# Softplus as one ScalarE operation, and one exponential over both halves of an attention tile

## The chip, the cores and the metric

One core of a Trainium2 chip runs the kernel. The metric is the device time of one execution in microseconds (us). Engines are named as in the profile: PE (TensorE, matrix products; PEld its weight loads), DVE (VectorE), ACT (ScalarE), POOL (GpSimd), SP (SyncE, which issues most DMAs).

## The reference

Windowed attention with 8 memory positions, then two dense layers over all 3072 tokens, all in fp32:

```python
for c in range(768 // 32):            # chunks of 32 queries, context 16 left, 8 right, and memory
    scores = scale * q_c @ k_full.T
    a = np.exp(scores - scores.max(-1))
    out_c = a / (a.sum(-1) + 1e-9) @ v_full
x = out.reshape(3072, 512)
h = x @ w_in                           # 512 x 2048
g = np.maximum(h, 0) + np.log1p(np.exp(-np.abs(h)))    # softplus
x = g @ w_out
h = x @ w_in2
g = np.maximum(h, 0) + alpha * np.minimum(h, 0)
return g @ w_out2
```

## The kernel before

**Tiling.** Attention works on 24 tiles of 128 tokens. A tile has two halves (`u` = 0, 1) of 64 queries; in each half the 8 heads lie as 4 pairs on 128 partitions, with 96 keys per query. The first dense layer goes over the tokens in 7 blocks of 4, 3, 3, 3, 4, 3 and 4 tiles (512 or 384 columns) and over the inner dimension in 16 pieces; a **step** is one piece of one block, 112 steps in all. The first two blocks each do the first 8 pieces before either does the second 8. The second dense layer follows, from about 700 us on, with a scheme of fewer products (`quad`, `out2`); the change doesn't touch it. fp32 products are made of three products of a rounded high part and a low part, so every operand is split: a cast on ACT writes the high part, a subtraction on DVE or POOL the low part.

**A step.** `pe_h` (L297) makes 12 products into a PSUM bank of `ps_h`, which has two. `act_first` (L312 to L321) computes softplus: on ACT the absolute value, the exponential and the logarithm (L312, L313, L318); the addition of one on ACT in the first 32 steps (L315) and on DVE later (L317); then three operations on DVE (L319 to L321), the last of which reads the PSUM bank again and so frees it. `act_split` casts (L328, ACT) and subtracts (L329, DVE); `pe_out` (L339) makes 12 products more into four accumulators.

**An attention tile.** `tile_plan` spreads a tile over six half-steps: scores of half 0 (products L197, then four reductions on DVE, L209, which also give the row's maximum); scores of half 1 beside the exponentials of half 0 (L219: 4 per half, on ACT, each with its sum); the norms (L228 to L230, DVE); the transposes (L237, PE, copied by ACT, L239); the values (L250, with the cast L256 and the subtraction L257). The score buffers `s` come from a pool of two; the first four tiles use space in the weight pool. The first block's four tiles run before the first step. The tiles of the second block start three half-steps apart, those of later blocks 7 or 11.

**Weights.** They come as float64 words. For each of 32 half pieces of a layer `conv_a` (L103, ACT) takes the absolute value of the high word, `conv_b` (L112, L113, L117, L120, DVE) builds fp32 from both words, and `split_w` casts (L129, ACT) and subtracts (L130, POOL). The first layer's conversions lie beside the first steps, the second layer's (`split_to`, L141, L142) from the third block on.

**Order.** Each function is put at a half-step by hand (`put`), and a scheduler orders each engine's queue from there by its own estimate of times; each engine then works its queue in order. An activation table that serves exponential and logarithm is loaded ahead of everything (L594).

Of the kernel before, what the change touches and what calls it, by code (L numbers as in the profile page):

```python
# [7 lines left out]
F32 = mybir.dt.float32  # L8
F32R = mybir.dt.float32r
I32 = mybir.dt.int32  # L10
# [6 lines left out]
P = 128  # L17
# [5 lines left out]
SW = 96  # L23
# [30 lines left out]
def attention_mlp_mlp_kernel(ctx: ExitStack, tc, qk, v, w1, w2, consts, out):  # L54
# [45 lines left out]

    def conv_a(layer, k, step=None):
        m = tpool.tile([P, DM], F32, tag="word", name="word", bufs=2)
        i = nc.scalar.activation(out=m, in_=raws[layer, k][:, :, 1].bitcast(F32), func=AF.Abs)  # L103
        pin(i, step)
        words[layer, k] = m

# [72 lines left out]
    def load_v(t):  # L179
        if t >= NT:  # L180
            return
        if t < BLOCKS1[0]:
            room = wpool.tile([P, 4 * DM], F32, tag="w", name="v0")
            v_t[t] = room[:SW, :2 * DM]
            s_room[t] = [room[:, 2 * DM + u * DM:][:, :NPAIR * SW].rearrange("p (g k) -> p g k", g=NPAIR) for u in range(2)]
        else:
            v_t[t] = apool.tile([SW, 2 * DM], F32, tag="v", name="v", bufs=1)
        nc.sync.dma_start(out=v_t[t], in_=v[t])

    def a_scores(t, u):  # L190
# [9 lines left out]
            )  # L200
        i = t % TPB
        m = mask[2 * u + (i == (TPB - 1 if u else 0))]
        if t < BLOCKS1[0]:
            s = s_room[t][u]
        else:
            s = apool.tile([P, NPAIR, SW], F32, tag="s", name="s_sb")
        nm = apool.tile([P, NPAIR], F32, tag="nm", name="nm")
        for g in range(NPAIR):
            nc.vector.tensor_tensor_reduce(  # L209
                out=s[:, g, :], in0=ps[:, g, :], in1=m, op0=ALU.add, op1=ALU.min,  # L210
                scale=-1.0 / float(D) ** 0.5, scalar=BIG, accum_out=nm[:, g:g + 1],
            )
        st[t, u] = (s, nm)

    def a_exp(t, u):
        s, nm = st[t, u]
        sm = apool.tile([P, NPAIR], F32, tag="sm", name="sm")
        for g in range(NPAIR):
            nc.scalar.activation(  # L219
                out=s[:, g, :], in_=s[:, g, :], func=AF.Exp, scale=-1.0,  # L220
                bias=nm[:, g:g + 1], accum_out=sm[:, g:g + 1],
            )
        st[t, u] = (s, sm)

    def a_norm(t, u):
        s, sm = st[t, u]
        r = apool.tile([P, NPAIR, 1], F32, tag="r", name="r")
        nc.vector.tensor_scalar(out=sm, in0=sm, scalar1=1e-9, scalar2=None, op0=ALU.add)  # L228
        nc.vector.reciprocal(out=r[:, :, 0], in_=sm)
        nc.vector.tensor_tensor(out=s, in0=s, in1=r.to_broadcast([P, NPAIR, SW]), op=ALU.mult)  # L230
        st[t, u] = s

    def a_transpose(t, u):
        s = st.pop((t, u))
        ps = ps_a.tile([SW, NPAIR, P], F32, tag="pa", name="ps_t")
        for g in range(NPAIR):
            nc.tensor.transpose(ps[:, g, :], s[:, g, :], ident)  # L237
        pt_t[t, u] = apool.tile([SW, NPAIR, P], F32, tag="pt", name="pt")
        nc.scalar.copy(out=pt_t[t, u], in_=ps)  # L239

# [18 lines left out]
    def tile_plan(t, b, c, first):  # L259

        plan = [
            (0, lambda: a_scores(t, 0)),
            (1, lambda: (a_exp(t, 0), a_scores(t, 1), load_qk(t + ahead(t)))),
            (2, lambda: (a_norm(t, 0), a_exp(t, 1))),
            (3, lambda: (a_transpose(t, 0), a_norm(t, 1))),
            (4, lambda: a_transpose(t, 1)),
            (5, lambda: (a_values(t, x_of(0, b), c), load_v(t + ahead(t)))),
        ]
        return [(first + s, f) for s, f in plan]

    def ahead(t):
        return 1 if t >= BLOCKS1[0] - 1 else NT
# [31 lines left out]
    def act_first(i):  # L304

        n = steps[i][4]
        ps = h_ps.pop(i)[:, :n]
        a = tpool.tile([P, N2], F32, tag="ta", name="ta", bufs=2)[:, :n]
        bt = tpool.tile([P, N2], F32, tag="tb", name="tb")[:, :n]
        lt = tpool.tile([P, N2], F32, tag="tl", name="tl")[:, :n]  # L310

        nc.scalar.activation(out=a, in_=ps, func=AF.Abs)  # L312
        nc.scalar.activation(out=a, in_=a, func=AF.Exp, scale=-1.0)  # L313
        if i < 2 * NF:
            nc.scalar.activation(out=bt, in_=a, func=AF.Identity, bias=1.0)  # L315
        else:
            nc.vector.tensor_scalar(out=bt, in0=a, scalar1=1.0, scalar2=None, op0=ALU.add)  # L317
        nc.scalar.activation(out=lt, in_=bt, func=AF.Ln)  # L318
        nc.vector.scalar_tensor_tensor(out=bt, in0=bt, scalar=-1.0, in1=lt, op0=ALU.add, op1=ALU.subtract)  # L319
        nc.vector.scalar_tensor_tensor(out=a, in0=bt, scalar=0.0, in1=a, op0=ALU.max, op1=ALU.subtract, reverse1=True)  # L320
        nc.vector.scalar_tensor_tensor(out=a, in0=ps, scalar=0.0, in1=a, op0=ALU.max, op1=ALU.add)  # L321
        g_a[i] = a

    def act_split(i):
# [266 lines left out]
    put(last + 28, lambda: load_w_out(1))  # L591
    put(last + 30, lambda: load_w_out(2))

    nc.scalar.preload_act_table_set("natural_log_exp_and_others")  # L594
    load_qk(0)
    load_raw(0, 0)
    nc.sync.dma_start(out=cst, in_=consts)
# [98 lines left out]
```

## Time and profile before

| | |
|---|---|
| median of 3 runs | 1202.24 us (1198.3 to 1203.86) |
| the profiled execution | 1200.04 us, its span 1198.3 us |
| mean granted clock of PE | 0.994 |
| first layer's first product, second layer's first product | about 32 us, about 650 us among the last steps |

Everything in the profile is read against the span of the one profiled execution. Busy time is the time in which an engine had an instruction; a busy share is an average over stages that have different limits. An idle time is put down to what ended last before the engine went on.

### The profile page before, as it was taken

The page shows a single profiled execution, that of the slowest core. Times are in us where ns is not written, and L with a number is a line of the kernel's source. Part 1 is how long each engine was busy: PE and PEld are TensorE (multiplying, and loading weights), DVE is VectorE, ACT ScalarE, POOL GpSimd, SP SyncE. Part 2 cuts the span into 40 slices and gives each one's busy share as a digit, 9 for nine tenths or more (in the row PEclk, how much of TensorE's full clock was granted, in tenths as well). Part 3 has the DMA queues.
Part 4 walks back from the last instruction along what each step waited for, and adds up shares of the span by engine and source line. Part 5 has one row for each costly group of instructions (what it writes and reads, how often), then busy time and mean ns, then how long its engine had stood idle before and what let it go on. Part 6 is the DMA issues. An engine that isn't in the chain of part 4 may idle for free.

```text
span 1198.3 us, 17139 instructions
## 1 busy us (share of the span) xinstructions
PE 1149.5 (96%) x6192; PEld 983.0 (82%) x6192; DVE 852.0 (71%) x1792; ACT 560.9 (47%) x1297; POOL 187.1 (16%) x148
## 2 busy tenths in 40 slices
PE   6898989989999999999999999999999999999997
PEld 6677868989999878899888888887888878888876
DVE  6999895878888888788868775567446565555542
ACT  7878665766766666566645521124121133211121
POOL 1232330323213212013212100003000002000000
PEclk9999999999999999999999999999999999999999
DMA  9554531475374362435313564465664493744630
GB/s 323 163 179 163 174 97 18 121 211 168 118 243 160 110 202 85 154 123 194 128 62 132 168 221 174 164 253 212 233 227 160 165 354 123 251 175 158 231 147 36
DMA packets 58661, 202.98 MB, mean 169 GB/s; under 512 B 5456, under 2 KB 10064, under 8 KB 52432
## 3 DMA queue, kind: packets, MB, share of 16 engines
q1 hardware_dynamic: 57424, 200.05, 48.5%
q0 software_dynamic: 1152, 1.84, 1.1%
q8 instruction: 49, 0.80, 0.3%
q14 instruction: 36, 0.29, 0.1%
HBM read 164.37 MB, written 37.49 MB: 168 GB/s over the span
## 4 chain that ended last, share of the span: by engine, by line
PE 45%; DMA 3%; DVE 2%; ACT 1%; SPq 0%; issue 0%; DVEq 0%; ACTq 0%
PE ps_o L450 20%; PE ps_q L425 18%; PE ps_hh L297 4%; PE ps_o L339 3%; DMA yraw<-y_dram 1%; DMA win<-w_in 1%; DMA out_dram<-o_sb 0%; DVE xop L401 0%; DVE ta L320 0%; DVE tp L433 0%; DVE tb L319 0%; ACT o_sb L358 0%; DVE tb L317 0%; DVE g L329 0%; SPq L382 0%
## 5 line engine op out<-in xcount | busy, mean ns | idle before, releaser
L297 PE MATMUL ps_hh<-x,wsplit 128*128 128x384 f32 (+1 forms) x1344 | 295.7, 368 | 17.1 <-DVE ta L321 15.3
L339 PE MATMUL ps_o<-g,wsplit 128*128 128x384 f32 (+1 forms) x1344 | 291.7, 362 | 3.2 <-DVE g L329 1.2
L450 PE MATMUL ps_o<-wout,g 128*128 128x512 f32 x1152 | 279.7, 392 | 3.8 <-ACT g L438 2.9
L297 PEld LDWEIGHTS ps_hh<-x,wsplit 128*128 128x128 f32 x1344 | 239.9, 190 | 46.1 <-DVE ta L321 19.6
L339 PEld LDWEIGHTS ps_o<-g,wsplit 128*128 128x128 f32 x1344 | 239.7, 188 | 27.7 <-DVE g L329 2.0
L450 PEld LDWEIGHTS ps_o<-wout,g 128*128 128x128 f32 x1152 | 216.2, 188 | 52.7 <-ACT g L438 5.4
L425 PE MATMUL ps_q<-xop,win 128*128 128x512 f32 x1008 | 245.4, 390 | 1.0 <-ACT tc L476 0.5
L425 PEld LDWEIGHTS ps_q<-xop,win 128*128 128x128 f32 x1008 | 189.2, 188 | 42.0 <-DVE xop L401 1.1
L438 ACT CAST g<-ta 128x512 fp32r<-128x512 f32 x48 | 29.9, 622 | 181.6 <-DVE ta L434 157.9
L319 DVE SCALAR_TENSOR_TENSOR tb<-tb,tl 128x384 f32<-128x384 f32 (+1 forms) x112 | 81.6, 729 | 24.6 <-ACT tl L318 23.7
L329 DVE TENSOR_TENSOR g<-ta,g 128x384 fp32r<-128x384 f32 (+1 forms) x112 | 72.5, 647 | 32.9 <-ACT g L328 32.4
L328 ACT CAST g<-ta 128x384 fp32r<-128x384 f32 (+1 forms) x112 | 62.1, 555 | 68.0 <-DVE ta L321 66.3
L320 DVE SCALAR_TENSOR_TENSOR ta<-tb,ta 128x384 f32<-128x384 f32 (+1 forms) x112 | 88.9, 794 | 1.9
L312 ACT ACTIVATE ta<-ps_hh 128x384 f32<-128x384 f32 (+1 forms) x112 | 59.4, 531 | 55.4 <-PE ps_hh L297 50.9
L318 ACT ACTIVATE tl<-tb 128x384 f32<-128x384 f32 (+1 forms) x112 | 63.6, 568 | 28.3 <-DVE tb L317 27.6
L439 DVE TENSOR_TENSOR g<-gb,g 128x512 fp32r<-128x512 f32 x48 | 34.6, 722 | 57.4 <-ACT g L438 57.4
L438 ACT CAST g<-gb 128x512 fp32r<-128x512 f32 x48 | 29.9, 622 | 92.6 <-PE ps_o L450 91.1
L433 DVE TENSOR_SCALAR tp<-ps_q,cst 128x512 f32<-128x512 f32 x48 | 35.9, 749 | 51.2 <-PE ps_q L425 51.2
L321 DVE SCALAR_TENSOR_TENSOR ta<-ps_hh,ta 128x384 f32<-128x384 f32 (+1 forms) x112 | 68.5, 611 | 2.3
L130 POOL TENSOR_TENSOR wsplit<-word,wsplit 128x512 fp32r<-128x512 f32 x32 | 50.4, 1576 | 125.2 <-ACT wsplit L129 125.2
L219 ACT ACTIVATE s_sb<-s_sb,nm 128x96 f32<-128x96 f32 x160 | 58.2, 366 | 15.8 <-DVE nm L209 15.3
L389 POOL TENSOR_TENSOR yt<-yraw 128x512 f32<-128x512 f32 x6 | 9.0, 1492 | 361.9 <-DVE xop L401 337.0
(62 smaller groups left out, 1243.9 us busy)
## 6 DMA issues: line engine op xcount, KB each, us to landing
wout<-w_out SPq DMA_DIRECT2D x48, 1024.0 KB, 6.2
raw<-in_w_dram SPq DMA_DIRECT2D x64, 512.0 KB, 4.2
win<-w_in SPq DMA_DIRECT2D x24, 1024.0 KB, 5.9
qk<-in_qk_dram SPq DMA_DIRECT2D x24, 832.0 KB, 5.1
win<-w_in SPq DMA_DIRECT2D x24, 768.0 KB, 6.4
w_in<-wst SPq DMA_DIRECT2D x24, 512.0 KB, 3.3
v<-in_v_dram SPq DMA_DIRECT2D x24, 384.0 KB, 4.8
w_out<-wst SPq DMA_DIRECT2D x16, 512.0 KB, 4.3
```

Of the source, the lines that this page charges most:

```text
L297: nc.tensor.matmul(ps[:, :n], lhsT=w[:, a, kc * P:(kc + 1) * P], rhs=x[:, c, kc, :], start=k == 0, stop=k == 3 * KD - 1,)
L312: nc.scalar.activation(out=a, in_=ps, func=AF.Abs)
L318: nc.scalar.activation(out=lt, in_=bt, func=AF.Ln)
L319: nc.vector.scalar_tensor_tensor(out=bt, in0=bt, scalar=-1.0, in1=lt, op0=ALU.add, op1=ALU.subtract)
L320: nc.vector.scalar_tensor_tensor(out=a, in0=bt, scalar=0.0, in1=a, op0=ALU.max, op1=ALU.subtract, reverse1=True)
L321: nc.vector.scalar_tensor_tensor(out=a, in0=ps, scalar=0.0, in1=a, op0=ALU.max, op1=ALU.add)
L328: anchor[i] = nc.scalar.copy(out=g[:, 0, :n], in_=a)
L329: nc.vector.tensor_tensor(out=g[:, 1, :n], in0=a, in1=g[:, 0, :n].bitcast(F32), op=ALU.subtract)
L339: nc.tensor.matmul(ps[:, :n], lhsT=w[:, a, DM + m * P:DM + (m + 1) * P], rhs=g[:, c, :n], start=first and k == 0, stop=final and k == 2,)
L425: nc.tensor.matmul(ps, lhsT=w[:, a, h * P:(h + 1) * P], rhs=x[:, c, h, :], start=first and k == 0, stop=k == 5, skip_group_check=not first,)
L438: nc.scalar.copy(out=g[:, 0, :], in_=a)
L450: nc.tensor.matmul(ps, lhsT=g[:, a, m * P:(m + 1) * P], rhs=w[:, c, :], start=f == 0 and k == 0, stop=f == NF - 1 and k == 2,)
```

## The change

`act_first` becomes one ACT operation (`Softplus`). A tile's two halves share one score buffer (of a pool of one) and one row of maxima: the maximum is now subtracted by DVE, one exponential on ACT covers both halves, one reduction on DVE makes the sums, and the norm is one chain for both. The absolute value of the weights' high word is made by two shifts on DVE. The preloading of the table is dropped. In the plan of a tile the exponential stands at half-step 2, the norm at 3 and both transposes at 4.

```diff
     def conv_a(layer, k, step=None):
         m = tpool.tile([P, DM], F32, tag="word", name="word", bufs=2)
-        i = nc.scalar.activation(out=m, in_=raws[layer, k][:, :, 1].bitcast(F32), func=AF.Abs)
+        i = nc.vector.tensor_scalar(
+            out=m.bitcast(I32), in0=raws[layer, k][:, :, 1], scalar1=1, scalar2=1,
+            op0=ALU.logical_shift_left, op1=ALU.logical_shift_right,
+        )
...
-            s_room[t] = [room[:, 2 * DM + u * DM:][:, :NPAIR * SW].rearrange("p (g k) -> p g k", g=NPAIR) for u in range(2)]
+            s_room[t] = room[:, 2 * DM:2 * DM + 2 * NPAIR * SW].rearrange("p (g k) -> p g k", k=SW)
...
-        if t < BLOCKS1[0]:
-            s = s_room[t][u]
-        else:
-            s = apool.tile([P, NPAIR, SW], F32, tag="s", name="s_sb")
-        nm = apool.tile([P, NPAIR], F32, tag="nm", name="nm")
+        if u == 0:
+            if t < BLOCKS1[0]:
+                s = s_room[t]
+            else:
+                s = apool.tile([P, 2 * NPAIR, SW], F32, tag="s", name="s_sb", bufs=1)
+            st[t] = s, apool.tile([P, 2 * NPAIR, 1], F32, tag="nm", name="nm")
+        s, nm = st[t]
...
-    def a_exp(t, u):
-        s, nm = st[t, u]
-        sm = apool.tile([P, NPAIR], F32, tag="sm", name="sm")
-        for g in range(NPAIR):
-            nc.scalar.activation(
-                out=s[:, g, :], in_=s[:, g, :], func=AF.Exp, scale=-1.0,
-                bias=nm[:, g:g + 1], accum_out=sm[:, g:g + 1],
-            )
...
+    def a_exp(t):
+
+        s, nm = st[t]
+        nc.vector.tensor_tensor(out=s, in0=s, in1=nm.to_broadcast([P, 2 * NPAIR, SW]), op=ALU.subtract)
+        nc.scalar.activation(out=s, in_=s, func=AF.Exp, scale=-1.0)
+
+    def a_norm(t):
+        s, _ = st[t]
+        sm = apool.tile([P, 2 * NPAIR], F32, tag="sm", name="sm")
+        r = apool.tile([P, 2 * NPAIR, 1], F32, tag="r", name="r")
+        nc.vector.tensor_reduce(out=sm, in_=s, axis=mybir.AxisListType.X, op=ALU.add)
         nc.vector.tensor_scalar(out=sm, in0=sm, scalar1=1e-9, scalar2=None, op0=ALU.add)
         nc.vector.reciprocal(out=r[:, :, 0], in_=sm)
-        nc.vector.tensor_tensor(out=s, in0=s, in1=r.to_broadcast([P, NPAIR, SW]), op=ALU.mult)
-        st[t, u] = s
+        nc.vector.tensor_tensor(out=s, in0=s, in1=r.to_broadcast([P, 2 * NPAIR, SW]), op=ALU.mult)
...
-            (1, lambda: (a_exp(t, 0), a_scores(t, 1), load_qk(t + ahead(t)))),
-            (2, lambda: (a_norm(t, 0), a_exp(t, 1))),
-            (3, lambda: (a_transpose(t, 0), a_norm(t, 1))),
-            (4, lambda: a_transpose(t, 1)),
+            (1, lambda: (a_scores(t, 1), load_qk(t + ahead(t)))),
+            (2, lambda: a_exp(t)),
+            (3, lambda: a_norm(t)),
+            (4, lambda: (a_transpose(t, 0), a_transpose(t, 1))),
...
-        bt = tpool.tile([P, N2], F32, tag="tb", name="tb")[:, :n]
-        lt = tpool.tile([P, N2], F32, tag="tl", name="tl")[:, :n]
-
-        nc.scalar.activation(out=a, in_=ps, func=AF.Abs)
-        nc.scalar.activation(out=a, in_=a, func=AF.Exp, scale=-1.0)
-        if i < 2 * NF:
-            nc.scalar.activation(out=bt, in_=a, func=AF.Identity, bias=1.0)
-        else:
-            nc.vector.tensor_scalar(out=bt, in0=a, scalar1=1.0, scalar2=None, op0=ALU.add)
-        nc.scalar.activation(out=lt, in_=bt, func=AF.Ln)
-        nc.vector.scalar_tensor_tensor(out=bt, in0=bt, scalar=-1.0, in1=lt, op0=ALU.add, op1=ALU.subtract)
-        nc.vector.scalar_tensor_tensor(out=a, in0=bt, scalar=0.0, in1=a, op0=ALU.max, op1=ALU.subtract, reverse1=True)
-        nc.vector.scalar_tensor_tensor(out=a, in0=ps, scalar=0.0, in1=a, op0=ALU.max, op1=ALU.add)
+        nc.scalar.activation(out=a, in_=ps, func=AF.Softplus)
...
-    nc.scalar.preload_act_table_set("natural_log_exp_and_others")
```

## Rows read from the trace of the kernel before

**Rows 1.** The page's first part: busy us, share of the span, instructions.

```profile
PE 1149.5 (96%) x6192; PEld 983.0 (82%) x6192; DVE 852.0 (71%) x1792; ACT 560.9 (47%) x1297; POOL 187.1 (16%) x148
```

**Rows 2.** Stretch, length; busy PE, PEld, DVE, ACT, POOL; PE's clock, DMA share, GB/s.

```profile
0.00:33.00 33.00, 22.84 (x241) 20.31 (x241) 23.35 (x118) 24.63 (x91) 4.02 (x7) 1.00 0.86 294
33.00:103.00 70.00, 63.51 (x415) 51.57 (x415) 69.63 (x185) 56.42 (x150) 22.36 (x15) 0.98 0.53 173
103.00:177.00 74.00, 63.74 (x343) 55.99 (x344) 68.98 (x141) 53.76 (x119) 24.25 (x15) 0.98 0.47 150
177.00:430.00 253.00, 246.63 (x1621) 229.54 (x1620) 205.89 (x511) 164.45 (x424) 61.11 (x55) 1.00 0.47 145
430.00:700.00 270.00, 266.04 (x1453) 227.07 (x1452) 213.19 (x424) 152.76 (x335) 57.14 (x45) 1.00 0.41 136
```

**Rows 3.** Waits of PE, 0 to 177 us, then 177 to 700: total, times, longest.

```profile
PE ps_hh L297 <- DVE ta L321: 8.8, 7, 2.2
...
PE ps_hh L297 <- DVE ta L321: 6.5, 9, 1.3
PE ps_x L250 <- ACT pt L239: 2.0, 1, 2.0
```

**Rows 4.** DVE by line and shape, 33 to 175 us: busy, mean ns, idle before.

```profile
L117 DVE SCALAR_TENSOR_TENSOR word<-raw,word 128x512 int32<-128x512 int32 x28 | 23.9, 854 | 0.2
...
L113 DVE TENSOR_SCALAR word<-word 128x512 int32<-128x512 int32 x27 | 14.4, 532 | 0.2
L320 DVE SCALAR_TENSOR_TENSOR ta<-tb,ta 128x512 f32<-128x512 f32 x12 | 10.8, 901 | 0.0
L319 DVE SCALAR_TENSOR_TENSOR tb<-tb,tl 128x512 f32<-128x512 f32 x12 | 10.3, 857 | 0.0
...
L321 DVE SCALAR_TENSOR_TENSOR ta<-ps_hh,ta 128x512 f32<-128x512 f32 x12 | 8.2, 680 | 0.0
L230 DVE TENSOR_TENSOR s_sb<-s_sb,r 128x384 f32<-128x384 f32 x12 | 7.7, 640 | 0.0
...
L320 DVE SCALAR_TENSOR_TENSOR ta<-tb,ta 128x384 f32<-128x384 f32 x8 | 6.6, 821 | 0.0
L321 DVE SCALAR_TENSOR_TENSOR ta<-ps_hh,ta 128x384 f32<-128x384 f32 x8 | 4.4, 548 | 0.0
L319 DVE SCALAR_TENSOR_TENSOR tb<-tb,tl 128x384 f32<-128x384 f32 x8 | 4.4, 547 | 0.0
...
L228 DVE TENSOR_SCALAR sm<-sm 128x4 f32<-128x4 f32 x12 | 2.5, 206 | 0.0
L229 DVE RECIPROCAL r<-sm 128x4 f32<-128x4 f32 x12 | 2.0, 168 | 0.0
```

**Rows 5.** All engines by line and shape, 0 to 33 us.

```profile
L219 ACT ACTIVATE v<-v,nm 128x96 f32<-128x96 f32 x32 | 11.6, 368 | 1.3 <-DVE nm L209 1.2
...
L112 DVE TENSOR_SCALAR word<-word 128x512 f32<-128x512 f32 x5 | 2.1, 420 | 8.8 <-ACT word L103 8.8
```

**Rows 6.** ACT by line and shape, 0 to 700 us.

```profile
L313 ACT ACTIVATE ta<-ta 128x384 f32<-128x384 f32 x64 | 33.5, 524 | 1.0
...
L313 ACT ACTIVATE ta<-ta 128x512 f32<-128x512 f32 x48 | 30.4, 632 | 0.9
...
L594 ACT ACT_TABLE_LOAD x1 | 1.3, 1283 | 0.7 <-PEq L686 0.7
```

**Rows 7.** Instructions in order of time, from 109 us: start, us, what.

```profile
109.09 0.66 DVE L117 SCALAR_TENSOR_TENSOR word<-raw,word 128x512 int32<-128x512 int32 x1
109.28 1.61 POOL L130 TENSOR_TENSOR wsplit<-word,wsplit 128x512 fp32r<-128x512 f32 x1 [5.46 <-ACT wsplit L129]
109.67 1.64 DVE L230 TENSOR_TENSOR s_sb<-s_sb,r 128x384 f32<-128x384 f32 x1
```

**Rows 8.** The same view, from 430 us: second half of one attention tile.

```profile
430.07 0.55 DVE L230 TENSOR_TENSOR s_sb<-s_sb,r 128x384 f32<-128x384 f32 x1
...
432.44 0.60 PE L237 MATMUL ps_t<-cst,s_sb 128*96 128x128 f32 x4
```

More of the change, by code (lines that the diff above doesn't have):

```diff
@@ L208, in a_scores @@
+        s, nm = st[t]
         for g in range(NPAIR):
+            k = u * NPAIR + g
             nc.vector.tensor_tensor_reduce(
-                out=s[:, g, :], in0=ps[:, g, :], in1=m, op0=ALU.add, op1=ALU.min,
-                scale=-1.0 / float(D) ** 0.5, scalar=BIG, accum_out=nm[:, g:g + 1],
-            )
-        st[t, u] = (s, nm)
-    def a_exp(t, u):
-        s, nm = st[t, u]
-        sm = apool.tile([P, NPAIR], F32, tag="sm", name="sm")
-        for g in range(NPAIR):
-            nc.scalar.activation(
-                out=s[:, g, :], in_=s[:, g, :], func=AF.Exp, scale=-1.0,
-                bias=nm[:, g:g + 1], accum_out=sm[:, g:g + 1],
-            )
-        st[t, u] = (s, sm)
@@ L225, in a_norm @@
-    def a_norm(t, u):
-        s, sm = st[t, u]
-        r = apool.tile([P, NPAIR, 1], F32, tag="r", name="r")
+                out=s[:, k, :], in0=ps[:, g, :], in1=m, op0=ALU.add, op1=ALU.min,
+                scale=-1.0 / float(D) ** 0.5, scalar=BIG, accum_out=nm[:, k, :],
+            )
+    def a_exp(t):
+        s, nm = st[t]
+        nc.vector.tensor_tensor(out=s, in0=s, in1=nm.to_broadcast([P, 2 * NPAIR, SW]), op=ALU.subtract)
+        nc.scalar.activation(out=s, in_=s, func=AF.Exp, scale=-1.0)
@@ L231, in a_norm @@
-        st[t, u] = s
+        nc.vector.tensor_tensor(out=s, in0=s, in1=r.to_broadcast([P, 2 * NPAIR, SW]), op=ALU.mult)
     def a_transpose(t, u):
-        s = st.pop((t, u))
+        s, _ = st[t] if u == 0 else st.pop(t)
         ps = ps_a.tile([SW, NPAIR, P], F32, tag="pa", name="ps_t")
         for g in range(NPAIR):
-            nc.tensor.transpose(ps[:, g, :], s[:, g, :], ident)
+            nc.tensor.transpose(ps[:, g, :], s[:, u * NPAIR + g, :], ident)
         pt_t[t, u] = apool.tile([SW, NPAIR, P], F32, tag="pt", name="pt")
```

## The prediction, made before the changed kernel had run

> **What bounds the kernel now.** I began with the busy shares of the page [rows 1]: TensorE (PE) is busy 96% of the span, VectorE (DVE) 71%, ScalarE (ACT) 47%. That average hides stages, so the next view is the busy time by stretch [rows 2], cut where the work changes: attention of the first block (to 33 us), conversion of the first layer's weights beside the first steps (to 177), the rest of the first layer (to 700), the second layer. PE is idle 33 - 22.84 = 10.2 us in the first stretch, 6.5 and 10.3 in the next two, 6.4 and 4.0 up to 700. The second layer has nothing that the change touches. So what can be won lies in 33 to 700 us and is 27.2 us of visible idle time, plus a little of the first stretch. DVE tells the stages apart: from 33 to 177 us it is busy 69.63 of 70 and 68.98 of 74 us, so there it is the bound; from 177 on it has about 50 us to spare in each row and only single waits cost PE time. The waits of PE name the culprit: the first product stands for a PSUM bank that the last softplus step on DVE (L321) has not yet freed, 8.8 us up to 177 and 6.5 after [rows 3].
>
> **The change part by part.** Sums are made against the profiled execution: span 1198.3, 1200.04 us in all. The median of the runs is 1202.24, 2.2 above it, within their spread.
>
> Softplus, 33 to 177 us. Per step three DVE operations go (L319 to L321) and four on ACT become one. In the stretch of [rows 4] these are 12 steps of 512 columns (10.8 + 10.3 + 8.2 = 29.3 us) and 8 of 384 (6.6 + 4.4 + 4.4 = 15.4): 44.7 us off DVE. The bank is then freed by one ACT operation of about 0.6 us (a 512-column ACT operation takes 632 ns [rows 6]) instead of by the last of seven on two queues. In these first steps the addition of one was on ACT, so nothing more leaves DVE there.
>
> Weight conversion. The absolute value of L103 moves to DVE as two shifts: 27 or so in this stretch. The trace does not have this operation. Its lower bound is the shift of L113, the same form on a packed source, 532 ns; its upper bound L117, which reads the same every-other-word source but two tensors, 854 ns [rows 4]. I take L113, because one source and one destination make it the nearer row: 27 x 0.53 = 14.4 us (23 at the upper bound). The wait for the raw weights moves with it: DVE already stood for L103 8.8 us in the first stretch [rows 5], so a wait is replaced and not added, and what is queued behind it on DVE (score reductions, norms) stood there before too.
>
> Attention. Per tile 8 exponentials with their accumulator reads become one. DVE gets a subtraction and a sum over 768 columns, its two normalising products become one of 768, its two pairs of small operations one pair. For 768 columns I extend L321: 680 ns at 512 and 548 at 384 [rows 4] give 1.03 ns a column, so 0.94 us each. Six tiles' worth lies in the stretch (12 of L230): subtraction and sum 6 x 1.88 = 11.3, product 6 x 0.94 - 7.7 = -2.1, small ones half of 2.5 + 2.0, -2.2. Together +7.0 us on DVE.
>
> So DVE's busy time falls by 44.7 - 14.4 - 7.0 = 23.3 us in a stretch that it bounds. This is the better end. The other end: durations in the rows overlap and hold collisions. L117 at 109.09 takes 0.66 but L230 begins 0.58 later, and that L230 takes 1.64 against a mean of 0.64 while GpSimd subtracts [rows 7]. GpSimd's 32 subtractions stay and will strike other operations. Counting the removed steps at 0.60 us for 512 columns and 0.47 for 384 (my estimate: the rows less 0.08 of overlap and the collisions) leaves 12 x 1.8 + 8 x 1.41 = 32.9 us removed, and with the upper bound of the shift 32.9 - 23 - 7 = 3 us gained. I take 14, about the middle, since each end rests on one of two unknowns falling one way. It can't pass the 16.8 us of visible idle time by much.
>
> First stretch, 0 to 33 us. There is no softplus here, only the added work: 5 conversions [rows 5] at 0.42 = 2.1 us, and for 4 tiles 4 x (1.88 + 0.94 - 2 x 0.64 - 0.37) = 4.7 us. DVE is busy 23.35 of the 26 us after the first data come. ACT is as full (24.63) and loses 32 exponentials at 368 ns [rows 5], but cannot give the time back, because each tile's chain now passes DVE twice more. Cost between 0 (some conversions can run later) and 6.8 us; I take 4, as the later weights still have to be converted.
>
> 177 to 700 us. DVE has room here, so the relief is worth only what PE's waits are: 10.4 us idle. The 6.5 us on L321 go. The wait for the transposes' copy (2.0 [rows 3]) stays, and waits of this kind may grow, since the tile's chain is longer by two DVE operations and both halves reach the transposes together. I take 6 gained, 0 to 10 as bounds.
>
> The rest. The score tile is one buffer of double size instead of two: a tile's score reductions must wait for the transposes of the one before. Only the second block's three tiles are planned closer (three half-steps apart) than a tile's six; behind the waiting reduction stand conversions and g's subtraction. I count this within the lower end above. The preloading of the activation table goes: its 1283 ns [rows 6] lie under the first loads, and a load put before the first exponential would cost at most that. No DMA changes its half-step.
>
> Sum: 4 - 14 - 6 = -16, so 1200.04 - 16 = 1184; with the median a little over the profiled run I say 1185.
>
> **The table rule.** The trace has a single table load, 1283 ns [rows 6]; all functions of the kernel before live in one set. The Trainium skill (ScalarE: Activation LUTs, Table sets: the hidden batching unit) says that functions are loaded in named sets and a change of set needs a load; it lists exponential and logarithm together and names no set with exponential and softplus. By its figure of 2.66 us for a switch, some 40 switches would be an estimated 106 us of ACT time. No run here shows yet which set softplus is in. The mechanism is the slower rival below. If it happens, 20 tiles lie between softplus steps, so 40 loads of 1.28 us by the row are 51 us; ACT is busy 57 to 73% of the stretches between 103 and 700 us [rows 2] and loses more than that with L313 alone (33.5 + 30.4 us [rows 6]), so its busy time does not decide, only its lateness.
>
> **The rivals.**
> A. DVE stops being the bound, and nearly all idle time between 33 and 700 us comes back: 27.2 less 4 gives 1177, and up to 10 us more where PE's matmuls now run stretched (clock 0.98 in two rows). For it: the busy-row ledger of 23 us. Against: collisions and the conversions stay. 1160 to 1177; chance 0.17.
> B. No change: the lower end of the ledger (3 gained, 6.8 lost at the start), and the later waits merely move from L321 to the transposes. About 1200, 1196 to 1208; chance 0.20. That softplus is built from several operations after all, so that little leaves the engines, ends here too (0.03 of it).
> C. Slower: PE stands at the transposes. They are placed in PE's queue early: in one tile the product ends at 430.62 and the transposes begin at 432.44, 1.8 us later [rows 8], and everything behind them (two products of a step) waits if they are late. The new chain is longer by subtraction and sum (1.88) and a table load (1.28), shorter by 4 x 0.37 - 0.85 for the exponentials (0.85 from the two sizes of L313 [rows 6]): 2.5 us. The scale tips where the lateness passes the 1.8 us of slack; 20 tiles at 0.7 us are 14 us, and 28 at twice that, with the reload for softplus behind it. From 1184 plus 14 to 28, and the start's cost at its upper end, 1208 to 1225. For it: the slack is small and DVE is a queue in order. Against: DVE and ACT are emptier, so the chain waits less in the queues. Chance 0.18.
>
> **How the numbers follow.** Forecast 0.45 (1177 to 1196, around 1185), A 0.17, B 0.20, C 0.18. A measurement of this kernel tells about 0.5%, 6 us, from no change: faster is under 1196, 0.45 + 0.17 = 0.62; same 0.20; slower 0.18. The range from 1167 to 1212 leaves out some four tenths of A and three quarters of C, 0.20.
>
> **What would show it.** Right: DVE busy in 33 to 177 us clearly below full and the waits on L321 gone with no wait of like size on softplus; the first block's first product a few us later than now; the shifts near 0.5 us; sum and subtraction near 0.95. Wrong: DVE still full to 177 us (B), transposes as PE's largest wait beside some 40 table loads (C), or the first layer's PE idle time gone (A).

## The result and the profile after

The change made the kernel slower: 1208.39 us (median of 5 runs, 1207.49 to 1211.79) against 1200.89 (5 runs, 1198.3 to 1203.86). The ratio on record is 1.0076 with an interval of 1.0052 to 1.0099; the two medians alone give 1.0062. That is 7.5 us more where 16 less were forecast; it lies inside the range, on the side that had a chance of 0.18. The profiled execution took 1211.79 us, the top of its runs, with a span of 1210.0.

The first part of the page of the changed kernel and, from its second part, the row of PE's granted clock in 40 slices (to be read against [rows 1]):

```profile
PE 1151.6 (95%) x6192; PEld 997.1 (82%) x6192; DVE 678.3 (56%) x1416; ACT 399.7 (33%) x656; POOL 172.0 (14%) x148
...
PEclk9698899979999999999999999999999999999999
```

The relief came: DVE has 174 us less to do, ACT 161. Yet PE is busy 2 us longer with the same 6192 products and idle 58.4 us, 9.6 more than before, and its clock is lower: the mean over the span is 0.972, against 0.994 before. The busy time by stretch, cut as in [rows 2] and with its columns, and then finer around the places where the loss sits:

```profile
0.00:33.00 33.00, 19.06 (x144) 17.54 (x144) 25.70 (x101) 9.50 (x14) 4.01 (x7) 0.89 0.87 293
33.00:103.00 70.00, 61.09 (x346) 49.23 (x347) 68.88 (x136) 28.75 (x46) 21.28 (x16) 0.88 0.44 145
103.00:177.00 74.00, 62.07 (x357) 56.22 (x356) 57.22 (x119) 29.38 (x49) 17.06 (x13) 0.86 0.43 141
177.00:430.00 253.00, 244.68 (x1657) 233.34 (x1657) 130.42 (x354) 109.49 (x180) 56.81 (x54) 0.97 0.46 142
...
20.00:34.00 14.00, 6.88 (x90) 6.10 (x89) 14.00 (x47) 5.20 (x9) 2.51 (x2) 0.70 0.72 226
34.00:52.00 18.00, 14.85 (x107) 11.97 (x106) 17.83 (x44) 6.57 (x12) 5.53 (x4) 0.59 0.48 164
104.00:126.00 22.00, 11.90 (x101) 10.05 (x101) 20.00 (x46) 8.87 (x14) 5.08 (x4) 0.66 0.58 194
126.00:244.00 118.00, 116.44 (x634) 107.06 (x634) 60.63 (x128) 42.33 (x73) 22.07 (x19) 0.98 0.31 85
244.00:268.00 24.00, 16.24 (x122) 14.49 (x121) 10.06 (x36) 9.74 (x15) 7.31 (x7) 0.72 0.77 210
```

Read it in two steps. In the coarse rows DVE is still full from 33 to 103 us and has air from 103 on (57.22 of 74, before 68.98). The fine rows show three holes, at 20 to 52, 104 to 126 and 244 to 268 us: PE is busy about half of the first 14 us and of the second hole, and the granted clock is 0.59 to 0.72. Between the second and third hole PE is nearly full (116.44 of 118) and DVE half empty. A *stand* is, from here on, a time in which an engine waits. What PE waited for over the whole execution, to be read against [rows 3] (total, times, longest):

```profile
PE ps_t L239 <- DVE s_sb L233: 12.1, 4, 6.2
...
PE ps_t L239 <- DVE v L233: 7.1, 2, 3.6
...
PE ps_hh L299 <- ACT ta L311: 0.6, 2, 0.5
```

The 15.3 us in which products stood for the softplus step L321 are gone, and softplus on ACT (L311) costs 0.6. In their place stand 19.2 us at the transposes (L239) for the normalising product (L233): `v` is the score space of the first block's tiles, `s_sb` the new single buffer. The instructions in order of time show the three holes. First PE and DVE in the first block, then all engines at the end of the second block's last tile, then the third block (start, us, engine, what, and in brackets the idle time before it and what ended it):

```profile
26.36 1.91 PE L239 MATMUL ps_t<-cst,v 128*96 128x128 f32 x8 [3.60 <-DVE v L233]
...
26.73 0.94 DVE L230 TENSOR_REDUCE sm<-v 128x8 f32<-128x768 f32 x1
...
29.06 0.67 DVE L123 SCALAR_TENSOR_TENSOR word<-raw,word 128x512 int32<-128x512 int32 x1
...
32.60 0.94 DVE L233 TENSOR_TENSOR v<-v,r 128x768 f32<-128x768 f32 x1
...
33.70 1.91 PE L239 MATMUL ps_t<-cst,v 128*96 128x128 f32 x8 [3.52 <-DVE v L233]
...
115.04 0.95 DVE L223 TENSOR_TENSOR s_sb<-s_sb,nm 128x768 f32<-128x768 f32 x1
115.79 1.28 ACT L224 ACT_TABLE_LOAD   x1
117.08 0.84 ACT L224 ACTIVATE s_sb<-s_sb 128x768 f32<-128x768 f32 x1
117.96 0.95 DVE L230 TENSOR_REDUCE sm<-s_sb 128x8 f32<-128x768 f32 x1 [1.37 <-ACT s_sb L224]
119.39 0.96 DVE L233 TENSOR_TENSOR s_sb<-s_sb,r 128x768 f32<-128x768 f32 x1
120.40 1.94 PE L239 MATMUL ps_t<-cst,s_sb 128*96 128x128 f32 x8 [6.23 <-DVE s_sb L233]
...
251.69 0.26 DVE L215 CUSTOM_DVE_ANT_0 s_sb<-ps_s,cst 128x96 f32<-128x96 f32 x1 [3.20 <-PE ps_t L239]
...
253.38 1.15 PE L252 MATMUL ps_x<-pt,v 96*64 96x64 f32 x32
...
259.79 1.94 PE L239 MATMUL ps_t<-cst,s_sb 128*96 128x128 f32 x8 [5.26 <-DVE s_sb L233]
...
261.66 1.98 PE L252 MATMUL ps_x<-pt,v 96*64 96x64 f32 x32
```

At the start one tile's sum begins at 26.73 and its product ends at 33.54: 6.8 us for four operations that last 2.2, because other work stands between them in DVE's queue: conversions (L123, at 29.06, and two more), the next tile's subtraction and sum, and the low parts of `x`. At 115 us the chain is bare: subtraction, table load, exponential, sum, norm, product, one after the other, and PE stands 6.23 us. At 251 us the single buffer shows itself: the reductions of the next tile (L215) stand 3.20 us until the transposes of the tile before have read `s_sb`, and then the bare chain again keeps PE for 5.26. The clock is in the last lines: the same 32 products of L252 take 1.15 us before this stand and 1.98 after it.

The same places in the kernel before, in the fine cut (its lines have the same columns):

```profile
20.00:34.00 14.00, 9.78 (x142) 8.14 (x141) 11.59 (x50) 12.04 (x43) 1.27 (x1) 1.00 0.75 228
34.00:52.00 18.00, 16.32 (x105) 13.36 (x105) 17.73 (x52) 15.96 (x47) 5.55 (x5) 0.91 0.66 228
...
104.00:126.00 22.00, 19.79 (x132) 18.24 (x133) 20.80 (x58) 17.94 (x51) 5.39 (x4) 0.92 0.55 185
...
244.00:268.00 24.00, 20.93 (x145) 19.97 (x144) 18.18 (x53) 13.85 (x40) 5.44 (x6) 1.00 0.86 222
```

A table of milestones, the starts of single products read from PE's rows in order of time (us), for the runs that the explanation uses. A step's end is given by the start of its last product, which lasts some 0.4 us:

| | first product | step 7, last | step 8, first | step 23, last | step 32, first | step 111, last |
|---|---|---|---|---|---|---|
| before | 32.3 | 112.1 | 94.5 | 204.8 | 235.8 | 699.4 |
| after | 45.3 | 106.7 | 125.9 | 212.6 | 265.3 | 709.5 |
| e1, two score buffers | 46.2 | 108.7 | 121.8 | 208.5 | 253.8 | 695.1 |
| e3, Softplus alone | 34.0 | 97.8 | 103.9 | 193.4 | 233.6 | 684.5 |
| e5, e1 with the old first block | 33.6 | 98.9 | 101.2 | 190.6 | 232.6 | 675.0 |
| e8, Exp and Ln, old attention | 33.9 | 94.7 | 99.7 | 185.1 | 227.0 | 666.8 |

Step 8 is the second block's first, and the kernel before begins it while step 7 still runs; step 32 is the third block's first. After starts 13.0 us late and has made that good by the end of step 7 (5.4 us ahead). It loses it again before step 8, which begins 31.4 us later than before, and before step 32 (29.5 later).

### The profile page after: what moved, and what is told of

Its sections match the earlier page's. It is cut to its first block, busy times and chain, and to the rows that moved or that the text cites. A ratio compares the mean times of both kernels' runs of the same rounds, so it can differ in the third digit from the quotient of the medians.

```text
span 1210.0 us, 16069 instructions
## 1 busy us (share of the span) xinstructions
PE 1151.6 (95%) x6192; PEld 997.1 (82%) x6192; DVE 678.3 (56%) x1416; ACT 399.7 (33%) x656; POOL 172.0 (14%) x148
## 4 chain that ended last, share of the span: by engine, by line
PE 75%; DVE 12%; DMA 8%; issue 2%; ACT 2%; POOL 1%; SPq 0%; ACTq 0%; POOLq 0%; DVEq 0%
PE ps_o L440 20%; PE ps_q L415 18%; PE ps_o L329 16%; PE ps_hh L299 16%; DMA yraw<-y_dram 2%; PE ps_s L200 2%; DMA w_in<-wst 2%; DVE word L120 2%; DVE word L115 2%; DVE word L123 2%; PE ps_x L252 1%; DVE word L116 1%; DVE word L103 1%; DMA y_dram<-o_sb 1%; PE ps_t L239 1%
## 5 line engine op out<-in xcount | busy, mean ns | idle before, releaser
L299 PEld LDWEIGHTS ps_hh<-x,wsplit 128*128 128x128 f32 x1344 | 246.7, 193 | 30.1 <-DVE x L259 4.8
L319 DVE TENSOR_TENSOR g<-ta,g 128x384 fp32r<-128x384 f32 (+1 forms) x112 | 77.0, 687 | 166.8 <-ACT g L318 166.7
L311 ACT ACTIVATE ta<-ps_hh 128x384 f32<-128x384 f32 (+1 forms) x112 | 60.2, 537 | 104.8 <-PE ps_hh L299 103.6
L200 PE MATMUL ps_s<-qk 128*128 128x96 f32 x384 | 59.0, 306 | 14.8 <-DMA qk<-in_qk_dram 8.0
L200 PEld LDWEIGHTS ps_s<-qk 128*128 128x128 f32 x384 | 55.6, 218 | 18.5 <-DMA qk<-in_qk_dram 6.9
L133 POOL TENSOR_TENSOR wsplit<-word,wsplit 128x512 fp32r<-128x512 f32 x32 | 43.4, 1357 | 137.4 <-ACT wsplit L132 137.4
L428 ACT CAST g<-gb 128x512 fp32r<-128x512 f32 x48 | 29.9, 623 | 94.5 <-PE ps_o L440 94.1
L145 POOL TENSOR_TENSOR wst<-word,wst 128x512 fp32r<-128x512 f32 (+1 forms) x32 | 39.5, 1235 | 128.2 <-ACT wst L144 128.2
L466 ACT COPY tc<-ps_q 128x512 f32<-128x512 f32 x48 | 28.2, 588 | 82.8 <-PE ps_q L415 80.1
L120 DVE SCALAR_TENSOR_TENSOR word<-raw,word 128x512 int32<-128x512 int32 x64 | 51.7, 808 | 1.3
```

The costliest lines, as they stand in the source:

```text
L120: nc.vector.scalar_tensor_tensor(out=mi, in0=r[:, :, 1], scalar=-0x40000000, in1=mi, op0=ALU.bitwise_and, op1=ALU.bitwise_or)
L133: lo_eng.tensor_tensor(out=w[:, 1, :], in0=m, in1=w[:, 0, :].bitcast(F32), op=ALU.subtract)
L145: nc.gpsimd.tensor_tensor(out=t[:, 1, :n], in0=src, in1=t[:, 0, :n].bitcast(F32), op=ALU.subtract)
L200: nc.tensor.matmul(ps[:, g, :], lhsT=src[:, (u * NPAIR + g) * P:(u * NPAIR + g + 1) * P], rhs=src[:, k0:k0 + SW], start=True, stop=True,)
L299: nc.tensor.matmul(ps[:, :n], lhsT=w[:, a, kc * P:(kc + 1) * P], rhs=x[:, c, kc, :], start=k == 0, stop=k == 3 * KD - 1,)
L311: nc.scalar.activation(out=a, in_=ps, func=AF.Softplus)
```

## The experiments

Nothing of the computation is left out in any of them; line numbers are each kernel's own. The theory was that the attention part loses, in two places (the start, the buffer), what Softplus gains; the rivals were the table loads and the work added to DVE.

**e1_two_buffers.** Two score buffers of double size; two scratch tiles of the second layer move to other space to make room.

```diff
-                s = apool.tile([P, 2 * NPAIR, SW], F32, tag="s", name="s_sb", bufs=1)
+                s = apool.tile([P, 2 * NPAIR, SW], F32, tag="s", name="s_sb", bufs=2)
...
-            t = tpool.tile([P, N2], F32, tag="tb", name="tc")
+            t = late["x"].tile([P, N2], F32, tag="tb", name="tc")
...
-        u2 = tpool.tile([P, N2], F32, tag="tl", name="u2")
+        u2 = late["x"].tile([P, N2], F32, tag="tl", name="u2")
```

> The changed kernel with two score buffers of 768 columns instead of one (two scratch tiles of the second layer move to another pool to make room). Theory 'buffer': the single score buffer holds the last tile of the second and third blocks back, so PE stands at steps 8 and 32 and its clock falls after it. Then the first product of step 8 starts within 5 us of the end of step 7's second products instead of 19 us after, no stand of over 3 us is left at step 32, and the time is 1184 to 1197 us. Theory 'tables': the 39 table loads delay each tile's exponential. They stay at about 39 here, so both gaps stay and the time is 1203 to 1212. Theory 'start': the loss is made by the fuller start alone; step 0 still ends about 9 us late and the time is 1200 to 1208.

Measured 1197.34 us (10 runs), 0.9967 of before (0.9944 to 0.999), 11.0 less than after. The stretch of the third hole and PE's waits:

```profile
244.00:268.00 24.00, 20.09 (x140) 19.46 (x139) 13.89 (x41) 11.72 (x18) 5.96 (x6) 0.93 0.88 255
...
PE ps_t L239 <- DVE s_sb L233: 10.7, 4, 7.2
```

The third hole is half filled (PE 20.09 us against 16.24), and step 32 begins 11.5 us earlier. The stand before step 8 is still there (7.2 us) and the start is as late as in after. So the buffer is one price, about 11 us, and the rest has another place: the time lies just over the 1197 that the theory 'buffer' allowed, and step 8 does not follow step 7 within the 5 us that it named. The mechanism shows at the third block's last tile. In after its scores are reduced from 251.69 us on, once the transposes of the tile before have read `s_sb`; here from 232.99 on, ahead of those transposes (e1, in order of time):

```profile
232.99 0.26 DVE L215 CUSTOM_DVE_ANT_0 s_sb<-ps_s,cst 128x96 f32<-128x96 f32 x1
...
234.74 0.60 PE L239 MATMUL ps_t<-cst,s_sb 128*96 128x128 f32 x4
```

**e2_abs_on_act.** The absolute value of the weights goes back to ACT, all else as in after.

```diff
-        i = nc.vector.tensor_scalar(
-            out=m.bitcast(I32), in0=raws[layer, k][:, :, 1], scalar1=1, scalar2=1,
-            op0=ALU.logical_shift_left, op1=ALU.logical_shift_right,
-        )
+        i = nc.scalar.activation(out=m, in_=raws[layer, k][:, :, 1].bitcast(F32), func=AF.Abs)
```

> The changed kernel with the absolute value of the weights' high word back on ACT; all else as changed. Theory 'start': the first product of step 0 comes 3 to 5 us earlier than 45.3 us, the half-clock stretch at the start gets shorter, and the time is 1198 to 1204. Theory 'buffer': the gaps at steps 8 and 32 stay (12 to 20 us and 8 to 14 us), and the time stays within 1203 to 1210. Theory 'tables': number of loads unchanged, 1205 to 1210.

Measured 1228.99 us, 1.0225 (1.0177 to 1.0273). None of the theories had this. Its table loads by line:

```profile
L308 ACT ACT_TABLE_LOAD x54 | 69.3, 1283 | 1.0
...
L103 ACT ACT_TABLE_LOAD x39 | 50.0, 1283 | 3.7 <-DMA raw<-in_w_dram 2.3 <-PEq L672 0.7
```

There are 108 loads where after has 40 (20 at softplus, 19 at the exponential, one at the start): the absolute value (L103) draws 38 of its own, beside the one at the start, softplus (L308) 54 and the exponential 15 (at L221). 68 loads more, and 20.6 us more, of which e10 below puts 5 on the place of the absolute value itself, if that price carries over. So this run does not price the shifts; it shows that the move of the absolute value off ACT belongs to the Softplus edit, and that loads do cost time once there are many.

**e3_softplus_only.** Softplus, the shifts and the dropped preload, on the attention of before (two halves, eight exponentials, plan of before).

```diff
-        nc.scalar.activation(out=a, in_=ps, func=AF.Abs)
...
-        nc.vector.scalar_tensor_tensor(out=a, in0=ps, scalar=0.0, in1=a, op0=ALU.max, op1=ALU.add)
+        nc.scalar.activation(out=a, in_=ps, func=AF.Softplus)
```

> Softplus as one operation and the shifts on DVE, but the attention of the kernel before: halves apart, two score buffers, four exponentials with their sums per half. Theory 'buffer': no gap at steps 8 and 32, the first product near 35 to 38 us, time 1178 to 1192. Theory 'tables': the exponentials of the halves stand apart, so up to 80 loads; the tiles come later than in the changed kernel and the time is over 1212. Theory 'start': the first product falls back to 33 to 38 us, and the gain is about the 9 us that step 0 was late: 1197 to 1202.

Measured 1184.81 us, 0.9869 (0.9817 to 0.9922), 17 us less than the kernel before in the runs beside it (1201.86), although 70 table loads run. The first product comes at 34.0 us. DVE by line and shape up to the first product, here:

```profile
L233 DVE TENSOR_TENSOR v<-v,r 128x384 f32<-128x384 f32 x8 | 4.7, 591 | 0.1
...
L103 DVE TENSOR_SCALAR word<-raw 128x512 int32<-128x512 int32 x5 | 2.5, 499 | 6.5 <-DMA raw<-in_w_dram 6.5
```

and in after, up to 45.3 us:

```profile
L103 DVE TENSOR_SCALAR word<-raw 128x512 int32<-128x512 int32 x7 | 4.0, 572 | 6.6 <-DMA raw<-in_w_dram 6.6
L223 DVE TENSOR_TENSOR v<-v,nm 128x768 f32<-128x768 f32 x4 | 3.8, 948 | 0.0
L233 DVE TENSOR_TENSOR v<-v,r 128x768 f32<-128x768 f32 x4 | 3.8, 947 | 0.0
L230 DVE TENSOR_REDUCE sm<-v 128x8 f32<-128x768 f32 x4 | 3.8, 942 | 0.0
```

The shifts cost the start 1.7 us (34.0 against 32.3), since DVE stood there for the same weights anyway [rows 5]. Subtraction, sum and product are 11.4 us in after, the product alone 4.7 here; and by its first product after has begun 7 conversions, where here it is 5: two more lie between the steps of the longer chain.

**e4_attention_only.** The attention part alone, with softplus, absolute value and preload of before; its diff is the change of the attention above.

> The attention of the changed kernel (one score buffer, one exponential for both halves) with the softplus of before, the absolute value on ACT and the table of before: one load. Theory 'buffer': the gaps at steps 8 and 32 are there without any table switch, and DVE is fuller: 1212 to 1235. Theory 'tables': one load, so the tiles are no later than before: 1196 to 1206. Theory 'start': the first product comes at 40 to 44 us, the rest as before: 1206 to 1212.

Measured 1236.43 us, 1.0287 (1.0243 to 1.0331): 34.6 us slower than the kernel before in the runs beside it, and just over the 1235 of the theory 'buffer'. DVE is still needed for softplus here, and PE's largest wait says so:

```profile
PE ps_hh L296 <- DVE ta L320: 24.5, 20, 4.1
```

It was 15.3 in the kernel before. On a DVE without room the added work costs more (34.6) than on the relieved one (after less e3: 23.6). The two parts are not additive, and the attention part has no gain of its own in either setting.

**e5_first_block_old.** e1, with the first block's four tiles on the attention of before (two halves, eight exponentials, its plan).

```diff
+        if t < BLOCKS1[0]:
+            plan = [
+                (0, lambda: a_scores_old(t, 0)),
+                (1, lambda: (a_exp_old(t, 0), a_scores_old(t, 1), load_qk(t + ahead(t)))),
+                (2, lambda: (a_norm_old(t, 0), a_exp_old(t, 1))),
+                (3, lambda: (a_transpose_old(t, 0), a_norm_old(t, 1))),
+                (4, lambda: a_transpose_old(t, 1)),
...
```

> The kernel with two wide score buffers, but the four tiles of the first block take the attention of the kernel before (halves apart, exponentials with their sums). Theory 'start and buffer' (of the attention's price, about 11 us is the single buffer and most of the rest is the first block, where each tile's longer chain stands alone and PE's clock falls): the first product of step 0 comes at 33 to 37 us instead of 46.2 us, and the time is 1184 to 1190. Rival 'chain everywhere' (the longer chain costs at the later blocks too): the start is earlier but steps 8 and 32 lose it again, 1192 to 1198.

Measured 1177.52 us, 0.9814 (0.978 to 0.9849): 19.8 us less than e1, more than was expected. The fine stretches:

```profile
20.00:34.00 14.00, 13.11 (x149) 11.36 (x146) 11.95 (x49) 9.17 (x31) 1.27 (x1) 0.76 0.74 231
34.00:52.00 18.00, 16.62 (x80) 13.50 (x80) 16.63 (x43) 8.34 (x13) 5.26 (x4) 1.00 0.47 145
...
104.00:126.00 22.00, 21.92 (x134) 21.60 (x133) 19.91 (x52) 12.47 (x21) 5.77 (x5) 1.00 0.58 195
```

PE is busy 13.11 of the 14 us up to 34, where after had 6.88, and at full clock from 34 to 52. The second hole has closed as well, so the start is worth 20 us and not the 13 by which the first product is late. The likeliest reading is that the late start had also pushed the second block's attention against its own first step.

**e6_halves_apart.** Subtraction by DVE, one exponential, sum and product for each half, in narrow buffers and the plan of before, with Softplus and the shifts. The plan alone, against after:

```diff
-            (1, lambda: (a_scores(t, 1), load_qk(t + ahead(t)))),
-            (2, lambda: a_exp(t)),
-            (3, lambda: a_norm(t)),
-            (4, lambda: (a_transpose(t, 0), a_transpose(t, 1))),
+            (1, lambda: (a_exp(t, 0), a_scores(t, 1), load_qk(t + ahead(t)))),
+            (2, lambda: (a_norm(t, 0), a_exp(t, 1))),
+            (3, lambda: (a_transpose(t, 0), a_norm(t, 1))),
+            (4, lambda: a_transpose(t, 1)),
```

> Softplus as one operation, shifts on DVE, and the attention with the changed operations (subtraction, one exponential, one reduction) but for each half by itself, with the plan and the two narrow score buffers of the kernel before. Theory 'gathering' (what costs is that both halves go as one unit through one buffer): first product at 35 to 40 us, no stand over 4 us at steps 8 and 32, 1185 to 1193. Rival 'DVE work' (the subtraction and the reduction on DVE cost, however they are cut): first product at 44 us or later, 1195 to 1204.

Measured 1197.62 us (10 runs), 0.9971 (0.995 to 0.9993), as the rival had it. The first product comes at 45.9 us, although nothing is gathered over two halves. So at the start the price is the subtraction and the sum that moved onto DVE, not the joining of the halves.

**e7_no_switches.** After, with softplus as two ACT operations that share one table with the attention's exponential.

```diff
-        nc.scalar.activation(out=a, in_=ps, func=AF.Softplus)
+        nc.scalar.activation(out=a, in_=ps, func=AF.Exp)
+        nc.scalar.activation(out=a, in_=a, func=AF.Ln, bias=1.0)
...
+    nc.scalar.preload_act_table_set("natural_log_exp_and_others")
```

> The changed kernel with softplus as two ACT operations, exponential and the logarithm of one plus it, both in the table of the kernel before, so one load instead of 39. Theory 'loads are hidden': gaps at steps 8 and 32 stay within 2 us of the changed kernel's, 1203 to 1211. Rival 'loads delay the tiles': each tile's chain is 1.3 us shorter, the gaps shrink by that and all waits behind a load go, 1185 to 1200.

Measured 1206.52 us (10 runs), 1.0051 (1.0032 to 1.0071). One load is left of 40, and 1.9 us are won, which the added logarithms may blur. PE's longest wait at the transposes is 7.1 us now:

```profile
PE ps_t L239 <- DVE s_sb L233: 13.5, 3, 7.1
```

So the loads are not what makes after slow; e4, which loses 34.6 us with a single load, says the same.

**e8_exp_ln_old_attention.** The kernel before with that same pair of ACT operations; attention, absolute value on ACT and preload untouched.

```diff
-        nc.scalar.activation(out=a, in_=ps, func=AF.Abs)
-        nc.scalar.activation(out=a, in_=a, func=AF.Exp, scale=-1.0)
...
-        nc.vector.scalar_tensor_tensor(out=a, in0=ps, scalar=0.0, in1=a, op0=ALU.max, op1=ALU.add)
+        nc.scalar.activation(out=a, in_=ps, func=AF.Exp)
+        nc.scalar.activation(out=a, in_=a, func=AF.Ln, bias=1.0)
```

> The kernel before with its softplus replaced by two ACT operations (exponential, logarithm of one plus it): attention, absolute value on ACT and the one table as before. If what pays is taking the softplus chain off DVE, this gives at least what softplus as one operation gave with the old attention, without shifts on DVE and without its 70 loads: 1172 to 1185. If ACT, with the absolute values, exponentials and two operations a step, becomes the late one instead: 1186 to 1198.

Measured 1167.15 us, 0.9732 (0.9692 to 0.9772): the fastest of all, 34 us under before and below the 1172 that was expected at best. In the last stretch before the second layer PE has no hole left:

```profile
430.00:700.00 270.00, 270.00 (x1508) 235.56 (x1507) 111.18 (x275) 127.25 (x296) 47.64 (x42) 1.00 0.44 148
```

It takes the exponential of the value itself and not of its negative magnitude, so it holds only while that fits into fp32 (up to about 88).

**e9_old_start_one_buffer.** e5 with one score buffer again (`bufs=1`).

> As the kernel whose first block keeps the old attention (1177.52 us), but with one wide score buffer for the other tiles, as in the changed kernel. If start and buffer are two prices that add, the buffer's 11 us come on top: stands of PE before steps 8 and 32 return, 1185 to 1192. Rival: the buffer only hurt because the start was late, 1175 to 1181.

Measured 1187.56 us, 0.9887 (0.985 to 0.9924): 10.0 us over e5. From 177 to 300 us one wait at the transposes is back:

```profile
PE ps_t L237 <- DVE s_sb L231: 5.3, 1, 5.3
```

The buffer costs 10.0 with the old start and 11.0 with the new one; the start costs 19.8 with two buffers and 20.8 with one (after less e9). Two prices that add.

**e10_no_switches_abs_on_act.** e7 with the absolute value back on ACT (the edit of e2).

> The changed kernel with softplus as exponential and logarithm (one table, 1206.52 us) and the absolute value of the weights' high word on ACT as before, so that the move of this operation is undone without any table load. Theory 'DVE work at the start': five or so shifts of 0.34 us less before the first product, which comes 1 to 3 us earlier than 46.1 us; with 32 fewer by 177 us the time is 1196 to 1204. Rival: the start is set by the tiles' own chain of DVE operations, 1204 to 1209.

Measured 1211.56 us, 1.0093 (1.0062 to 1.0125): outside both expectations, 5 us slower than e7. The absolute values in ACT's queue:

```profile
L103 ACT ACTIVATE word<-raw 128x512 f32<-128x512 f32 x64 | 43.0, 672 | 49.7 <-DMA raw<-in_w_dram 26.0 <-POOL wsplit L130 19.7 <-POOL wsum L152 3.2
```

ACT stands there for the raw weights and for GpSimd. By the end of step 23 this kernel is 2 us ahead of e7, and at the end of step 111 4.1 behind (710.9 against 706.8 us). In between, from 177 to 710 us, PE waits 3.9 us for ACT's casts of `x` and 3.4 for its copies of the transposes, where e7 has 0.7 and 0.2. That the stands before the absolute values make those casts and copies late is the likeliest reading, no more.

**e11_combined.** e5 with exponential and logarithm, absolute value on ACT and the preload: all that seemed best.

> First block with the old attention, the other tiles gathered with two wide buffers, softplus as exponential and logarithm, absolute value on ACT, one table. The kernel with the old attention throughout took 1167.15 us. If gathering pays in the later blocks (as 1177.52 against 1184.81 us suggests): 1158 to 1165. If that difference came from saved table loads: 1165 to 1172.

Measured 1176.04 us, 0.9814 (0.9759 to 0.9869): slower than either expectation, 8.9 over e8, which differs in the gathered attention of the later blocks alone (and the place of two scratch tiles). The loss arises behind step 23: by the end of step 23 the two are 0.6 us apart (185.7 against 185.1), by the end of step 111 10.4 (677.2 against 666.8). PE's waits from 177 to 700 us, the two largest totals here, then the largest of e8:

```profile
PE ps_hh L355 <- ACT x L304: 3.8, 3, 2.6
PE ps_x L298 <- ACT pt L236: 2.0, 4, 1.1
...
PE ps_t L237 <- ACT ta L310: 1.0, 1, 1.0
```

All of them together are 10.5 us here and 1.7 in e8, a difference as large as the loss; 5.8 of the 10.5 are for ACT's casts of `x` and copies of the transposes, as in e10. What makes these late was not tested.

**e12_exp_ln_shift.** e8 with the shifts on DVE.

> As the kernel that took 1167.15 us (old attention, softplus as exponential and logarithm, one table), but with the shifts on DVE instead of the absolute value on ACT: the one move alone. If the shifts cost on DVE's full early stretch: first product within 2 us of 33.9 us, step 23 ends 4 to 9 us later than 185.1 us, 1170 to 1178. Rival (what freed ACT brings is worth as much, as with the gathered attention, where the absolute value on ACT cost 5 us): 1160 to 1168. Against softplus as one operation with the same rest (1184.81 us, 70 loads) it also gives the price of those loads: 7 to 15 us by the first, over 17 by the second.

Measured 1172.22 us, 0.9748 (0.9722 to 0.9774), as the first theory had it. Against e8 the shifts cost 5.1 us in all. Against e3, which differs in one Softplus for Exp and Ln (and the preload), 12.6 us go with the 69 loads that are gone.

The account in medians: before 1200.9; Softplus with the shifts to 1184.8 (e3); gathering in the later blocks with two buffers to 1177.5 (e5, -7.3); the first block too, to 1197.3 (e1, +19.8); one buffer, 1208.4 (after, +11.0). The gain of 7.3 in the later blocks comes where it also saves table loads; without loads to save (e8 to e11) the same step lost 8.9. But the pairs differ in a second thing, the place of the absolute value: DVE in e3 and e5, ACT in e8 and e11. On ACT it cost 5.0 us beside the gathered attention (e10 against e7) and saved 5.1 beside the old one (e8 against e12). If these prices carry over, they are 10 of the 16.2 us between the pairs, and some 6 are left for the loads; no run tests the two apart.

## Why the prediction was wrong

**Right: the relief of DVE.** Softplus with the shifts gives 17 us (e3), about what was forecast for the whole change; the waits on L321 went, and nothing of like size took their place on softplus. The prices of the operations held. From the groups by line (busy, mean ns, idle before), over the whole execution and then for the shifts in 33 to 175 us:

```profile
L224 ACT ACTIVATE s_sb<-s_sb 128x768 f32<-128x768 f32 x20 | 16.9, 847 | 6.0 <-DVE s_sb L223 5.7
...
L311 ACT ACT_TABLE_LOAD x20 | 25.7, 1283 | 0.3
L224 ACT ACT_TABLE_LOAD x19 | 24.4, 1283 | 0.3
...
L103 DVE TENSOR_SCALAR word<-raw 128x512 int32<-128x512 int32 x27 | 12.4, 457 | 0.2 <-DMA raw<-in_w_dram 0.2
```

The shift takes 457 ns (532 taken), the exponential 847 (0.85 us taken), sum, subtraction and product 942 to 948 at the start (0.94 taken).

**The step that failed first: "First stretch ... I take 4", between 0 and 6.8.** The added work was counted well: 4.7 us on DVE, and up to the first product the groups of sum, subtraction, product and small operations are 12.8 us in after and 8.2 in e3, 4.6 apart. But the first product came 13.0 us later, and e5 shows the whole price as 20. The term priced work and not the chain. DVE was full (14.00 of 14 us), its queue put conversions and the next tile's operations between the steps of a tile's norm, 2.2 us of operations took 6.8, and PE stood twice for over 3.5 us. Its clock fell, to 0.70 from 20 to 34 us and 0.59 from 34 to 52 (e5: 0.76 and 1.00); and the lateness met, as e5 makes likely, the second block's tiles, whose bare chain made the stand of 6.23 us before step 8. e6 puts the late start on the two operations moved to DVE.

**The step that failed next: "Only the second block's three tiles are planned closer", counted "within the lower end".** The third block's tiles are three half-steps apart as well (L555 of the kernel before gives the blocks up to number 2 half the room), which this step and the description of the plan both missed. The single buffer costs 10 to 11 us (e1, e9), most of it there: in the profiled executions after ends step 111 14.4 us behind e1, and 10.3 of them arise behind step 23. A tile can't be scored before the one before it is transposed, so the room that DVE has from 126 to 244 us (busy 60.63 of 118) doesn't help the last tile, whose whole chain then stands bare before step 32.

**Missing from the sum: the clock.** It stood at 1.00 or 0.98 in every row of [rows 2], and no term of the sum let it fall. If only the two levels are granted, a mean of 0.972 is some 68 us of the span at 1.2 GHz (1210.0 x 0.028 / 0.5), 0.994 some 14. The four transposes of [rows 8] took 0.60 us; eight took 1.91 to 1.94 after the stands. How much of the two prices is the clock's and how much the stands' own was not measured apart. The first product's lateness is repaid by step 7; the stands at the seams are not.

**The other terms.** By the milestones of the profiled executions after loses 13.0 us to the first product (4 taken), gains 5.2 from there to the end of step 23 (14 taken for 33 to 177 us), loses 2.3 from there to the end of step 111 (6 gained taken) and 1.6 in the second layer (nothing taken). With Softplus and the shifts alone (e3) the gain to step 23 is 13.1, so the 14 was about right but for the attention part. "6 gained, 0 to 10" from 177 to 700 us: between the ends of steps 23 and 111 after takes 496.9 us and before 494.6, but e1 takes 486.6, 8 gained, and e5 484.4. The term was right for two buffers. That the range took the time in is due to its width; the sum had the wrong sign.

**The rivals.** C had the place (the transposes) and, at its edge, the time (1208 to 1225); its cause was wrong. It built on a slack of 1.8 us and on the table loads. There are 40 of them, as it said, but they cost about 2 us (e7). Nor do its bounds follow from its terms: 1184 plus 14 to 28, and 2.8 more at the start, is 1201 to 1215. C's rule, that of the Trainium skill (ScalarE: Activation LUTs, Table sets: the hidden batching unit), that a change of set needs a load, is borne out where functions alternate: 68 loads more cost e2 some 16 us (20.6 less the 5 of e10), 69 more than in e12 cost e3 12.6. The figure of 2.66 us for a switch, which the same page of the Trainium skill gives (What ACT_TABLE_LOAD costs), does not show here: a load takes 1283 ns, and the function behind the one at 115.79 begins 0.01 us after its end. B was as near: it said that the waits would move from L321 to the transposes, and they did (15.3 to 19.2 us); its 6.8 us for the start were about half of the 13.0. A's times (1160 to 1177) were reached by e8, e11 and e12 and all but reached by e5 (1177.52), once the first block's attention was left alone.

## What to carry to other kernels

A change with several parts is best priced part by part: here one part gives 17 us and the other takes 24, and the sum looks like a small loss. Work that was moved onto a full engine cost here by where it stood in a chain, not by its duration: look for the places where the chain is bare, at the start and where a block begins, and count what the engine's queue puts between its steps. When two operations are joined, their buffer doubles in size; if it becomes one instead of two, the slack that the plan counted on has gone.

## What the hardware showed that was not expected

PE's clock fell to the lower level around stands of 3.5 to 6 us: the stretches of 14 to 24 us around them have a granted clock of 0.59 to 0.72, and in the third hole the same 32 products take 1.15 us before the stand and 1.98 after it. In the second hole the clock had fallen before the long stand: these products take 1.98 us already at 112.20, when PE had been busy 4.33 of the 8 us from 104 on. Beside Softplus even the absolute value on ACT drew table loads of its own (38 at L103 in e2). Softplus as one operation isn't the fastest here: exponential and logarithm, 112 operations more on ACT, beat it by 12.6 us (e12 against e3), with one table load and not 70.
